# Decode attention and GLU on one core: whole-tile loads of K and V, an 80 KB K buffer with alternating places, and filler products on TensorE

## The chip, the cores and the metric

The kernel runs on one core of a Trainium2 chip. The metric is the device time of one execution in microseconds (us). The core has five engines that run their own instruction streams and wait for one another through semaphores: TensorE (PE in the profile; PEld is its weight load), VectorE (DVE), ScalarE (ACT), GpSimd (POOL) and SyncE (SP), which here issues nearly all of the transfers from HBM to SBUF. Sixteen DMA engines carry the transfers.

## The reference

One decode step of a transformer block, for one token with 640 features (bf16):

```python
h  = x + attention(layernorm(x)) @ wo       # 32 heads of 128, 4096 cached keys and values per head
h2 = h + (gelu(ln(h) @ w_gate) * (ln(h) @ w_up)) @ w_down      # hidden width 1728
```

`attention` computes q = layernorm(x) @ wq, the scores q.k / sqrt(128) against each head's 4096 cached keys, a softmax, and the weighted sum of the cached values. K and V are 32 x 4096 x 128 bf16 each, 33.6 MB, so that the two caches make up 67 of the 84 MB that the kernel reads. Each value is used once.

## The kernel before

**Tiles.** The 32 heads are worked on in four tiles (j = 0 to 3, `NG = 4`) of eight heads. In a tile every one of the 128 partitions holds 256 consecutive rows (keys) of one head, 64 KB; sixteen partitions make one head. A tile has two halves (s = 0, 1) of 128 rows, and each half two quarters (i = 0, 1) of 64 rows. `HALF` is the number of elements of a half in one partition.

**Buffers.** `k_all` holds one K tile: 64 KB in each partition. `v_all` holds one V tile. The weights share these two buffers: wq lies in `v_all` at the start; after the caches, `wo` lies at the start of `k_all` and w_down (`wd_sb`) behind it, w_gate and w_up in `v_all`.

**The order on SP.** Transfers are issued by SP in a list that is written out by hand, each behind its own wait: wq; K0 in two halves; V0 (when the q projection has read wq); then per tile the next K's first half (when `mults[j, 0, 1]`, the second multiplication of this tile, has read the first half), its second half (when `mults[j, 1, 1]` has), and the next V (when `pvs[j, 1]`, the last product with this V, is done). V3 is issued in two halves. Behind them come wo in two halves of 2.6 MB (when `mults[3, 1, 1]` is done), eight small loads into `wd_lo`, w_gate (when `pvs[3, 1]` is done), w_up, and w_down in four pieces.

**A tile on the engines.** q is broadcast to all partitions in `qb`. `mult(j, s, i)` multiplies a quarter of K with q on VectorE (L393, 64 x 128 products per partition, written to `prod[:, i]`). `fold(e, i)` lets TensorE add up groups of eight products by sixteen products with the identity `id_b` (L369 and, with the weights left loaded, the helper `held`, L167); i = 0 fills two PSUM banks, i = 1 two others. `total(j, s)` reduces the remaining sixteen on VectorE (L399) to the scores `sc`; ScalarE takes the exponential (L401) to `pt`; `block(j, s)` spreads it on VectorE to a block-diagonal weight `p_bd` (L406); `pv(e, s)` multiplies with V by 32 products (L381). Folds alternate between the two halves of `prod`, so the third multiplication waits for the first fold, and the third fold for the first reduction, which frees its PSUM banks.

VectorE's order in a tile is: mult, mult, mult, total, mult, block, total, block. TensorE's is a hardware loop over the tiles: `f00`, `f01`, `f10`, `f11`, `p0`, `p1`, `h`. Here `p0` waits for the first `p_bd` half and for V, `p1` for the second `p_bd` half and for `seen[j]`, a one-element memset on GpSimd (L437) that waits for V's second part; `h` sums over the partitions of a head (L387), after ScalarE's copy L443.

**The end.** After the last `h` the softmax sums are applied (L452 to L458), then the output projection with wo runs as two groups of 80 one-column products (L486), one for each half of wo; then the second layernorm, gate and up (L516, 75 one-column products each), the gelu chain on VectorE (L522 to L530), and the product with w_down (L539). At the start of TensorE's stream and near the end of VectorE's, `idle` puts NoOps (56 and 3).

The softmax here doesn't subtract the row's maximum and nothing guards it: scores larger than these inputs give would overflow.

## Time and profile before

| what | us |
|---|---|
| median of 3 runs (lowest, highest) | 202.18 (202.15, 202.31) |
| the profiled execution: its time | 202.28 |
| its span, first to last instruction | 200.9 |
| TensorE busy / VectorE busy / ScalarE busy | 115.3 / 103.6 / 9.4 |
| transfers: 84.23 MB, mean rate | 419 GB/s |
| mean granted TensorE clock | 0.795 |

A page's row gives a group of instructions: its line, engine, what it writes from what, how many there are and how long one takes, and how long the engine had been idle before them and what ended that. In a timeline a line has the start, the time from the first to the last of the merged instructions, the engine and the line, and in brackets the idle time before it. The chain of waits follows the work that ended last back to the start, and is printed in order of time.

### The profile page before, as it was taken

The numbers are of one execution on the slowest core, as the hardware profiler recorded it, in microseconds if no ns is written. First come the engines' busy times: TensorE is split into PE (matmuls) and PEld (weight loads), VectorE is DVE, ScalarE is ACT, GpSimd is POOL, SyncE is SP. The second block draws the span as 40 slices with busy tenths as digits, with TensorE's granted clock in tenths as the row PEclk, the third lists the DMA queues.
The fourth block names the chain that finished last, engine by engine and source line by source line (L and its number), as shares of the span: only waits on it lengthen the run. The fifth ranks groups of instructions, "written<-read, shape, count | busy, mean of one in ns | idle before, by whom it ended". The sixth has DMA issues, their size and how long they took to land.

```text
span 200.9 us, 2025 instructions
## 1 busy us (share of the span) xinstructions
PE 115.3 (57%) x982; PEld 30.4 (15%) x738; DVE 103.6 (52%) x56; ACT 9.4 (5%) x27; POOL 6.7 (3%) x36
## 2 busy tenths in 40 slices
PE   0108019667094296696605938566088496674675
PEld 0103000000032000001300000023000001474574
DVE  0200197994601969945149799420798965120320
ACT  2100000000001000000100000001000000100100
POOL 6500000000000000000000000000000000000000
PEclk9999856999858559579965899969669879955555
DMA  8999999999899999999999999899999999999992
GB/s 326 449 406 437 431 450 424 417 431 499 385 444 417 424 522 417 417 417 411 417 424 424 489 457 444 378 411 424 424 450 437 431 444 391 432 436 414 423 402 107
DMA packets 3275, 84.31 MB, mean 420 GB/s; under 512 B 387, under 2 KB 582, under 8 KB 966
## 3 DMA queue, kind: packets, MB, share of 16 engines
q1 hardware_dynamic: 3266, 84.23, 97.8%
q8 instruction: 4, 0.07, 0.1%
q14 instruction: 1, 0.01, 0.0%
q10 hardware_dynamic: 4, 0.00, 0.0%
HBM read 84.23 MB, written 0.00 MB: 419 GB/s over the span
## 4 chain that ended last, share of the span: by engine, by line
DMA 66%; DVE 22%; PE 11%; issue 0%; ACT 0%; SPq 0%; DVEq 0%
DMA k_all<-in_A_k_cache_dram 56%; DVE prod L393 18%; DMA v_all<-in_B_w_up_dram 10%; PE psum L167 7%; DVE sc L399 3%; PE psum L516 1%; PE psum L539 1%; PE psum L381 1%; DVE p_bd L406 1%; PE psum L369 1%; SPq L59 0%; ACT pt L401 0%; ACT out_row L555 0%; DVE hm L530 0%; DVEq L114 0%
## 5 line engine op out<-in xcount | busy, mean ns | idle before, releaser
L393 DVE TENSOR_TENSOR prod<-k_all,qb 128x8192 bf16<-128x8192 bf16 x16 | 70.4, 4421 | 38.0 <-DMA k_all<-in_A_k_cache_dram 33.1
L167 PE MATMUL psum<-prod,id_b 128*128 128x512 bf16 x240 | 66.0, 437 | 0.0
L369 PE MATMUL psum<-prod,id_b 128*128 128x512 bf16 x16 | 7.3, 454 | 45.3 <-DVE prod L393 31.5
L381 PE MATMUL psum<-v_all,p_bd 128*32 128x512 bf16 x256 | 19.4, 464 | 14.2 <-DMA v_all<-in_A_v_cache_dram 11.0
L399 DVE TENSOR_REDUCE sc<-psum 128x128 f32<-128x2048 f32 x8 | 18.3, 2288 | 13.3 <-PE psum L167 13.3
L369 PEld LDWEIGHTS psum<-prod,id_b 128*128 128x128 bf16 x16 | 1.6, 99 | 99.8 <-DVE prod L393 59.4
L381 PEld LDWEIGHTS psum<-v_all,p_bd 128*32 128x32 bf16 x256 | 7.5, 114 | 38.5 <-DMA v_all<-in_A_v_cache_dram 21.8
L406 DVE TENSOR_TENSOR p_bd<-pt,own 128x1024 bf16<-128x1024 bf16 x8 | 9.8, 1222 | 2.2 <-ACT pt L401 2.2
L401 ACT ACTIVATE pt<-sc,zero_t 128x128 bf16<-128x128 f32 x8 | 3.2, 402 | 135.9 <-DVE sc L399 135.9
L352 PE MATMUL psum<-v_all,xlnB 128*32 128x512 bf16 x40 | 4.5, 631 | 6.7 <-DMA v_all<-in_A_wq_dram 6.7
L486 PE MATMUL psum<-aP,k_all 128*128 128x1 bf16 x160 | 6.7, 178 | 2.7 <-DMA k_all<-in_A_wo_dram 2.7
L486 PEld LDWEIGHTS psum<-aP,k_all 128*128 128x128 bf16 x160 | 6.6, 131 | 2.8 <-DMA k_all<-in_A_wo_dram 2.8
L516 PE MATMUL psum<-hlnT,v_all 128*128 128x1 bf16 x150 | 5.5, 173 | 1.2 <-DMA v_all<-in_B_w_up_dram 1.2
L387 PE MATMUL psum<-hs,po_sb 128*128 128x8 f32 x32 | 4.2, 258 | 3.2 <-ACT po_sb L443 3.2
L437 POOL MEMSET spare<- 1x1 f32 x4 | 0.4, 88 | 162.8 <-DMA v_all<-in_A_v_cache_dram 162.8
L361 DVE CAST qb<-psum 128x512 bf16<-128x512 f32 x1 | 0.7, 692 | 9.7 <-PE psum L352 9.7
L516 PEld LDWEIGHTS psum<-hlnT,v_all 128*128 128x128 bf16 x150 | 5.3, 120 | 1.8 <-DMA v_all<-in_B_w_up_dram 1.3
L492 DVE COPY hT<-psum 128x5 f32<-128x5 f32 x1 | 0.2, 166 | 9.6 <-PE psum L486 9.6
L387 PEld LDWEIGHTS psum<-hs,po_sb 128*128 128x128 f32 x32 | 3.9, 191 | 5.1 <-issue 5.1
L323 PE MATMUL psum<-one_bf,x_row 1*128 1x1 bf16 x5 | 0.4, 177 | 7.1 <-DMA x_row<-in_A_x_dram 7.1
L326 DVE COPY xx<-psum 128x5 f32<-128x5 f32 x1 | 0.2, 165 | 7.5 <-PE psum L323 7.5
L443 ACT COPY po_sb<-psum 128x512 f32<-128x512 f32 x4 | 2.3, 585 | 22.3 <-PE psum L381 22.3
(71 smaller groups left out, 28.6 us busy)
## 6 DMA issues: line engine op xcount, KB each, us to landing
k_all<-in_A_k_cache_dram SPq DMA_DIRECT2D x8, 4096.0 KB, 29.1
v_all<-in_A_v_cache_dram SPq DMA_DIRECT2D x2, 4096.0 KB, 28.5
v_all<-in_A_wq_dram SPq DMA_DIRECT2D x1, 5120.0 KB, 15.2
k_all<-in_A_wo_dram SPq DMA_DIRECT2D x2, 2560.0 KB, 17.4
v_all<-in_B_w_gate_dram SPq DMA_DIRECT2D x1, 2160.0 KB, 15.0
v_all<-in_B_w_up_dram SPq DMA_DIRECT2D x1, 2160.0 KB, 19.8
k_all<-in_B_w_down_dram SPq DMA_DIRECT2D x1, 800.0 KB, 22.3
k_all<-in_B_w_down_dram SPq DMA_DIRECT2D x1, 640.0 KB, 20.9
```

Source lines behind the costliest of these rows:

```text
L167: built = e.matmul(out, lhsT, rhs, start=start, stop=stop)
L352: i = e.matmul(ps_q[32 * t:32 * t + 32, :], xlnB[:, c, 32 * a:32 * a + 32], wq_j[:, c, t, a, :, :], start=(c == 0 and a == 0), stop=(c == ...
L369: mm = held if n or not first else lambda e, *a, **k: e.matmul(*a, **k)
L381: i = e.matmul(ps_o[a:a + 32, :], p_bd[:, s, 4 * b:4 * b + 4, :].rearrange("p g j -> p (g j)"), vt[:, 4 * b:4 * b + 4, :], start=(s == 0 a ...
L387: i = e.matmul(ps_a[:, bass.ds(at, 8)], po_sb[:, 128 * r:128 * r + 128], hs[:, r, :], start=(r == 0), stop=(r == 3))
L393: mults[j, s, i] = VM(lambda e: e.tensor_tensor(out=prod[:, i, :, :], in0=kt[:, 64 * i:64 * i + 64, :], in1=qb[:, j, :].unsqueeze(1).to_br ...
L399: reds[j, s] = VR(lambda e: e.reduce_sum(sc[:, :], ps_f.rearrange("p (g d) -> p g d", d=16), axis=AX.X), folds[j, s, 1], exps.get((j, 0) i ...
L401: exps[j, s] = AS(lambda e: e.activation(pt[:, :], sc[:, :], ACTF.Exp, bias=zero_t[:, 0:1], scale=INV_SQRT_DH, accum_out=RS[:, 2 * j + s:2 ...
L406: blocks[j, s] = VB(lambda e: e.tensor_tensor(out=p_bd[:, s, :, :], in0=pt[:, :].unsqueeze(2).to_broadcast([128, 128, 8]), in1=own8[:, :]. ...
L443: evs[j] = AS(lambda e: e.copy(po_sb[:, :], ps_o), pvs[j, 1])
L486: r = e.matmul(ps_p[:, c:c + 1], wo_sb[:, i, c::5], aP[:, i:i + 1], start=False, stop=(i == 31), skip_group_check=True)
L516: i = e.matmul(ps[:, m:m + 1], ws, hlnT[:, c:c + 1], start=(c == 0 and m == 0), stop=(c == 4), skip_group_check=True)
```

## The change

- `k_all` becomes 80 KB in each partition. A K tile is loaded whole, in one transfer of 64 KB per partition: even tiles to rows 0 to 255 of the buffer, odd ones to rows 64 to 319. It is issued when the third multiplication of the tile before is done.
- Even tiles take their quarters in the order 2, 3, 1, 0, odd ones 0, 1, 2, 3, so that after three quarters all that the next tile overwrites has been read. In even tiles the second half's reduction is therefore two instructions of half the size.
- Every V tile is one transfer, the last one too, issued after the last V product of the tile before. The memsets `seen` go, and `p0` and `p1` run together after the second `p_bd`.
- `warm` adds products of a zero tile to a PSUM bank that is free: 8 when a K tile has landed, 12 between the second and the third fold, and 14 between the fourth fold and the products with V. They are 512 columns wide.
- wo is issued after the second multiplication of the last tile, instead of the last one.
- The NoOps on TensorE go from 56 to 22, those on VectorE go.

```diff
-    k_all = sb("k_all", [128, 2 * 128 * DH], BF16)
+    k_all = sb("k_all", [128, 320 * DH], BF16)
...
-    def load_k(j, s):
+    K_AT = [0, 64 * DH, 0, 64 * DH]
+
+    def load_k(j):
         src = A_k_cache[0, 8 * j:8 * j + 8, :, :].rearrange("h (p r) d -> (h p) (r d)", p=16)
-        landed["K", j, s] = P.dma("sync", k_all[:, HALF * s:HALF * s + HALF], src[:, HALF * s:HALF * s + HALF],
-                                  mults.get((j - 1, s, 1)))
+        landed["K", j] = P.dma("sync", k_all[:, K_AT[j]:K_AT[j] + 2 * HALF], src, mults.get((j - 1, 1, 0)), chan="K")
...
+    def load_v(j, *after):
+        landed["V", j] = P.dma("sync", v_all[:, 0:2 * HALF], src, *after, chan="V")
...
-    idle("tensor", 56)
+    idle("tensor", 22)
...
+    def warm(e, n, load=False):
+        for k in range(n):
+            mm = e.matmul if load and k == 0 else lambda *a, **kw: held(e, *a, **kw)
+            r = mm(ps_z, none_b[:, :], none_b[:, :].unsqueeze(1).to_broadcast([128, 4, 128]), start=True, stop=True)
         return r
...
     def mult(j, s, i):
-        kt = tile3(k_all[:, HALF * s:HALF * s + HALF])
+        c = (2 * s + i) if j % 2 else (2 + i, 1 - i)[s]
+        kt = tile3(k_all[:, K_AT[j]:K_AT[j] + 2 * HALF])
...
-            landed["K", j, s], qa, folds.get((j, 0, i) if s else (j - 1, 1, i)))
+            landed["K", j], qa, folds.get((j, 0, i) if s else (j - 1, 1, i)))
...
+        if s and j % 2 == 0:
+            V(lambda e: e.reduce_sum(sc[:, 64:128], g16(0, 1024), axis=AX.X), folds[j, s, 1], free)
+            reds[j, s] = VR(lambda e: e.reduce_sum(sc[:, 0:64], g16(1024, 2048), axis=AX.X))
+        else:
+            reds[j, s] = VR(lambda e: e.reduce_sum(sc[:, :], g16(0, 2048), axis=AX.X), folds[j, s, 1], free)
...
     lp = P.loop("tensor", range(NG), [
+        ("wa", lambda e, j: warm(e, 8, True), lambda j: [landed["K", j]], False),
         ("f00", lambda e, j: fold(e, 0), lambda j: [mults[j, 0, 0], reds[j - 1, 1] if j else qa], True),
         ("f01", lambda e, j: fold(e, 1), lambda j: [mults[j, 0, 1]], True),
+        ("wb", lambda e, j: warm(e, 12), lambda j: [], False),
         ("f10", lambda e, j: fold(e, 0), lambda j: [mults[j, 1, 0], reds[j, 0]], True),
         ("f11", lambda e, j: fold(e, 1), lambda j: [mults[j, 1, 1]], True),
-        ("p0", lambda e, j: pv(e, 0), lambda j: [blocks[j, 0], landed["V", j, 0]], True),
-        ("p1", lambda e, j: pv(e, 1), lambda j: [blocks[j, 1], seen[j]], True),
+        ("wc", lambda e, j: warm(e, 14), lambda j: [], False),
+        ("p0", lambda e, j: pv(e, 0), lambda j: [blocks[j, 1], landed["V", j]], True),
+        ("p1", lambda e, j: pv(e, 1), lambda j: [], True),
...
     for j in range(NG):
         mult(j, 0, 0)
         mult(j, 0, 1)
+        mult(j, 1, 0)
         if j < NG - 1:
-            load_k(j + 1, 0)
-        mult(j, 1, 0)
+            load_k(j + 1)
         total(j, 0)
         mult(j, 1, 1)
-        if j < NG - 1:
-            load_k(j + 1, 1)
         block(j, 0)
         total(j, 1)
         block(j, 1)
...
-        seen[j] = GS(lambda e: e.memset(spare[:, :], 0.0), landed["V", j, 1])
+        if j < NG - 1:
+            load_v(j + 1, pvs[j, 1])
...
-    d_wo = [... mults[NG - 1, 1, 1])
+    d_wo = [... mults[NG - 1, 0, 1])
             for i in (0, 16)]
...
-    idle("vector", 3)
```

## The prediction

> **What bounds the kernel now.** I read the page first (transfers, then the chain), then the timeline of the last tile, because the whole-span shares hide where a limit changes.

> The page's transfer rows and its queue table:

> ```profile
> DMA  8999999999899999999999999899999999999992
> q1 hardware_dynamic: 3266, 84.23, 97.8%
> ```

> The 16 engines are busy in every slice but the last; 84.23 MB are the whole input. The chain of waits says the same near its end (start, duration, what):

> ```profile
> 124.58 27.28 DMA k_all<-in_A_k_cache_dram
> ...
> 151.88 4.42 DVE prod L393
> 156.30 2.21 DVE sc L399
> ...
> 173.61 0.34 SPq L59
> ...
> 173.99 19.78 DMA v_all<-in_B_w_up_dram
> ```

> The last K half lands at 151.85; a compute path leads from there to the release of v_all (173.61), where the gate load is issued; then a transfer sets the pace again. Next the timeline, which shows how much room that compute path has:

> ```profile
> 142.17 8.76 DVE L393 TENSOR_TENSOR prod<-k_all,qb 128x8192 bf16<-128x8192 bf16 x2 [9.82 <-DMA k_all<-in_A_k_cache_dram]
> ...
> 151.88 4.42 DVE L393 TENSOR_TENSOR prod<-k_all,qb 128x8192 bf16<-128x8192 bf16 x1 [0.95 <-DMA k_all<-in_A_k_cache_dram]
> 156.22 2.29 DVE L399 TENSOR_REDUCE sc<-psum 128x128 f32<-128x2048 f32 x1
> 158.42 4.42 DVE L393 TENSOR_TENSOR prod<-k_all,qb 128x8192 bf16<-128x8192 bf16 x1
> ...
> 171.66 1.91 PE L381 MATMUL psum<-v_all,p_bd 128*32 128x512 bf16 x32 [2.42 <-DVE p_bd L406]
> 173.61 0.34 SPq L59 DMA_DIRECT2D v_all<-in_B_w_gate_dram  x1
> ...
> 177.53 3.33 PE L486 MATMUL psum<-aP,k_all 128*128 128x1 bf16 x80
> 183.53 3.36 PE L486 MATMUL psum<-aP,k_all 128*128 128x1 bf16 x80 [2.67 <-DMA k_all<-in_A_wo_dram]
> ...
> 193.82 2.75 PE L516 MATMUL psum<-hlnT,v_all 128*128 128x1 bf16 x75 [1.21 <-DMA v_all<-in_B_w_up_dram]
> ```

> The first two multiplications of tile 3 run at 142.17 on the first half of K, before the second half lands. After the last product with V (173.57) the rest waits only twice for a transfer: 2.67 us for the second half of wo and 1.21 us for up. So **the compute path at the end has 3.9 us of room**; without those waits it takes 27.3 (173.57 to the span's end, 200.9) - 3.9 = 23.4 us.

> [...] A full-clock fold of 16 products takes 3.62 us (0.216 each); at 0.5 ten take 4.00 us.

> **The change part by part**, for the last tile first. All bytes and their order in the queue stay, so the whole K3 lands when its second half did, at 151.85. What moves is tile 3's first two multiplications: they now wait for the whole tile, 9.71 us later. The new path, each duration from the rows above (two multiplications in 8.76, so 4.38 each in a row; a reduction 2.20 to the next start):

> - mult 1, 2, 3: 151.88 + 3 x 4.38 = 165.02. The third needs fold 1, which runs from 156.4 and at full clock ends at 160.0, before mult 2 does (160.64).
> - reduction 165.02 to 167.22, mult 4 to 171.64. Fold 3 (167.3 to 171.0) is hidden under it.
> - from a fourth mult's end to its p_bd, warm, tile 2 gives the time:

> ```profile
> 120.13 4.42 DVE L393 TENSOR_TENSOR prod<-k_all,qb 128x8192 bf16<-128x8192 bf16 x1
> ...
> 124.61 0.39 PE L369 MATMUL psum<-prod,id_b 128*128 128x512 bf16 x1 [0.64 <-DVE prod L393]
> 124.83 3.40 PE L167 MATMUL psum<-prod,id_b 128*128 128x512 bf16 x15
> 128.27 2.29 DVE L399 TENSOR_REDUCE sc<-psum 128x128 f32<-128x2048 f32 x1 [2.59 <-PE psum L167]
> ...
> 131.12 1.22 DVE L406 TENSOR_TENSOR p_bd<-pt,own 128x1024 bf16<-128x1024 bf16 x1 [0.56 <-ACT pt L401]
> ```

>  124.55 to 132.34 is 7.8 us: p_bd is done at 179.4.
> - Both V halves now follow it: 0.14 + 2 x 1.91 = 4.0 us, end 183.4. Before, p0 ran ahead of the last reduction; 1.9 of the delay is this.

> So v_all is free at 183.4 instead of 173.57: **9.8 us later**, against 3.9 us of room. Then 23.4 us: span 206.8 for 200.9, **+5.9 us**.

> Transfers at the end: the gate load, and everything queued behind it on SP (up, four w_down loads), is issued at 183.45. The second wo half lands about then (183.5), so the engines, which ran on, now pause. The output's own small DMA takes 1.0 us from issue to landing; with the completion of wo as much again, I estimate a pause of 1.5 to 3 us. Gate, up and w_down follow their old spacing (188.6, 193.8, 198.9), 2 us later: 190.6, 195.8, 200.9. Compute wants them at 197, 199.9 and 203.5. **The pause is hidden**; up to 2.6 us more would be too.

> Middle tiles, if the queue is never empty there: K(j+1) is issued 13.2 us after K(j) lands (three multiplications), V(j) lands 19.4 us after it. V(j+1) is issued 31.6 us after K(j), K(j+1) lands after 39. Room of 6 and 7 us; a cold first fold takes 2. So I cost them at nothing; the cover is the transfer already queued.

> Fills: no row shows products with the zero tile; price per piece 0.216 (full) to 0.43 (half), by the folds. Fill a (8) takes 3.4 us cold, under mult 1 (4.4). Fill b (12) 2.6 us, from 164.3 to 166.9, just before fold 3 at 167.3. Fill c (14) 3.0 us, 175.2 to 178.2, before p0 at 179.5. Warm, they delay nothing. Their worth is the clock: at best, every fold as above. At worst they do not raise it: fold 1 up to 2.1 later, fold 3 past mult 4 by 1.2, fill c 1.7 over, V products 6.5 (as at 54.92) instead of 3.9, +7.6 together. I take the full clock, and 0.3 for a late rise in fold 1.

> At nothing: two reductions for one in even tiles (about 0.1 us more, under the room above); 34 fewer NoOps on TensorE (the projection waits for wq until 15.27, xlnB is done at 10.1); the three NoOps on VectorE (its copy waited 2.42 anyway); the POOL memsets and five SP issues that go (no engine's bound); wo's earlier release (V3 is still ahead in the queue until 171.3); V3 in one piece (needed at 179.5).

> **Sum.** Span 200.9 + 5.9 + 0.3 = 207.1. The profiled execution took 202.28 with its span of 200.9, so 208.5; it stood 0.1 above the median of 202.18: **208.4**.

> **The rivals.**
> - *Fills do not hold the clock* (0.12). For: their operand is zero, and no row shows what counts as busy. Against: the gaps that they fill are where it fell. +2 to +7.6 on the sum: 210 to 216, middle 212.
> - *The clock stays up in the tail* (0.08). Output projection, GLU and down products (6.7, 5.5, 2.3 us) ran at 0.5; the projection now runs as one 6.7 us burst. All at double speed saves 7.2 us, but then w_down's landing at 200.9 sets the end, plus 2.0 us as before: 204.3. Against: 75 one-column products in a row left the clock at 0.5.
> - *A transfer gap in the middle* (0.05): a cold tile eats the 6 us room and K or V is issued late; +1 to +3, 209.5 to 211.5.
> - *Faster transfers, so not slower* (0.05). Whole-tile loads move faster and K3 lands earlier. It decides from 6 us, a landing at 145.9: 63.96 MB at 440 GB/s instead of 422, giving 202 or a little less. [...]
> - The forecast (0.70): 207.3 to 209.6.

> **How the numbers follow.** The likeliest case gives 208.4. The range runs from 206.5 (part of the tail fast) to 211.5 (middle gaps, fills half effective), leaving out the worst of the fills and the two low ends. A measurement here tells apart about 0.2%, 0.4 us; the only case near or below that is the fourth: faster 0.03, same 0.02, slower 0.95.

> **What would show it.** In the new profile: tile 3's first multiplication at 151.9 and none before; four of them with one reduction between; the last V product near 183.4; no transfer wait before the output projection; DMA below 9 tenths near 183 to 186; gate and up landed before their products. Wrong if K3 lands elsewhere than 151 to 153, if folds of the last tile take over 4.5 us (clock), if the one-column products take under 35 ns each, or if an engine waits for K for over 40 us between tiles.

## The result, and the profile after

The changed kernel takes **208.83 us** (median of 6 runs, 207.41 to 209.44) against 202.22 us before (6 runs, 202.15 to 202.31): 1.032 times as long, 95% interval 1.028 to 1.035. It is slower by 6.6 us. The profiled execution took 208.79 us with a span of 207.5.

The page of the changed kernel, its transfer rows and the queue:

```profile
DMA  9999999999999999999999999999999999839980
q1 hardware_dynamic: 2546, 84.23, 94.8%
```

The same 84.23 MB; the slices are full up to the 34th, then there is a hole in the next two, and the last slice carries next to nothing. The transfers no longer run to the end. The chain of waits of the changed kernel, its last part (start, duration, what):

```profile
125.98 25.55 DMA k_all<-in_A_k_cache_dram
...
151.56 4.44 DVE prod L400
...
156.65 4.97 PE psum L167 x15
...
161.64 4.43 DVE prod L400
...
180.45 3.67 PE psum L384 x64
...
188.02 6.46 PE psum L496 x160
...
197.49 5.28 PE psum L526 x150
...
202.81 0.46 issue
203.27 0.18 DVE hm L540
```

From the landing of K3 to the end there is no transfer in it any more. Before, a transfer of 19.8 us, up behind gate, stood in the chain shortly before the end; now the output projection (L496) runs its 160 products in one piece, gate and up (L526) their 150. The timeline of tile 3 shows where the time went:

```profile
151.56 8.76 DVE L400 TENSOR_TENSOR prod<-k_all,qb 128x8192 bf16<-128x8192 bf16 x2 [11.21 <-DMA k_all<-in_A_k_cache_dram]
...
156.44 5.16 PE L167 MATMUL psum<-prod,id_b 128*128 128x512 bf16 x15
...
161.64 4.43 DVE L400 TENSOR_TENSOR prod<-k_all,qb 128x8192 bf16<-128x8192 bf16 x1 [1.32 <-PE psum L167]
...
168.18 4.42 DVE L400 TENSOR_TENSOR prod<-k_all,qb 128x8192 bf16<-128x8192 bf16 x1
...
180.45 3.64 PE L384 MATMUL psum<-v_all,p_bd 128*32 128x512 bf16 x64 [1.15 <-DVE p_bd L419]
184.13 0.34 SPq L59 DMA_DIRECT2D v_all<-in_B_w_gate_dram  x1
```

All four multiplications stand behind K3's landing, where before two had been done by then. The third waited 1.32 us for the first fold, which ran mostly at half clock (granted clock 0.50 in the window from 156 to 160; 16 products in 5.6 us instead of 3.6). The gate load is issued at 184.13 instead of 173.61: 10.5 us later.

### The profile page after: what moved, and what is told of

It is laid out like the page before. It is cut to its first block, busy times and chain, and to the rows that moved or that the text cites. A ratio compares the mean times of both kernels' runs of the same rounds, so it can differ in the third digit from the quotient of the medians.

```text
span 207.5 us, 2113 instructions
## 1 busy us (share of the span) xinstructions
PE 139.0 (67%) x1118; PEld 29.7 (14%) x742; DVE 103.6 (50%) x58; ACT 9.4 (5%) x27; POOL 7.4 (4%) x32
## 3 DMA queue, kind: packets, MB, share of 16 engines
q1 hardware_dynamic: 2546, 84.23, 94.8%
HBM read 84.23 MB, written 0.00 MB: 406 GB/s over the span
## 4 chain that ended last, share of the span: by engine, by line
DMA 53%; DVE 27%; PE 18%; issue 1%; ACT 1%; SPq 0%; DVEq 0%
DMA k_all<-in_A_k_cache_dram 53%; DVE prod L400 23%; PE psum L167 7%; PE psum L496 3%; PE psum L526 3%; DVE sc L412 2%; PE psum L384 2%; PE psum L547 1%; PE psum L366 1%; DVE p_bd L419 1%; PE psum L390 1%; DVE hX L510 0%; PE psum L506 0%; PE psum L327 0%; ACT po_sb L453 0%
## 5 line engine op out<-in xcount | busy, mean ns | idle before, releaser
L167 PE MATMUL psum<-prod,id_b 128*128 128x512 bf16 x240 | 58.4, 399 | 0.0
L167 PE MATMUL psum<-none_b 128*128 128x512 bf16 x132 | 36.2, 430 | 0.0
L373 PE MATMUL psum<-none_b 128*128 128x512 bf16 x4 | 2.4, 608 | 30.9 <-DMA k_all<-in_A_k_cache_dram 30.9
L384 PE MATMUL psum<-v_all,p_bd 128*32 128x512 bf16 x256 | 14.5, 380 | 4.7 <-DVE p_bd L419 4.7
L412 DVE TENSOR_REDUCE sc<-psum 128x128 f32<-128x2048 f32 x6 | 13.7, 2286 | 5.2 <-PE psum L167 5.2
L366 PE MATMUL psum<-prod,id_b 128*128 128x512 bf16 x16 | 6.6, 415 | 10.1 <-DVE prod L400 7.8
L384 PEld LDWEIGHTS psum<-v_all,p_bd 128*32 128x32 bf16 x256 | 6.5, 97 | 37.1 <-DVE p_bd L419 30.9
L455 POOL TENSOR_TENSOR RT<-RS,own 128x64 f32<-128x64 f32 x1 | 1.3, 1325 | 170.9 <-ACT pt L413 170.9
L496 PE MATMUL psum<-aP,k_all 128*128 128x1 bf16 x160 | 6.6, 178 | 0.0
L496 PEld LDWEIGHTS psum<-aP,k_all 128*128 128x128 bf16 x160 | 6.5, 131 | 0.0
L526 PE MATMUL psum<-hlnT,v_all 128*128 128x1 bf16 x150 | 5.3, 173 | 0.0
L526 PEld LDWEIGHTS psum<-hlnT,v_all 128*128 128x128 bf16 x150 | 5.2, 120 | 0.5 <-DVE hlnT L513 0.5
L409 DVE TENSOR_REDUCE sc<-psum 128x64 f32<-128x1024 f32 x2 | 2.4, 1224 | 5.2 <-PE psum L167 5.2
## 6 DMA issues: line engine op xcount, KB each, us to landing
v_all<-in_B_w_up_dram SPq DMA_DIRECT2D x1, 2160.0 KB, 13.8
```

Source lines behind the costliest of these rows:

```text
L167: built = e.matmul(out, lhsT, rhs, start=start, stop=stop)
L366: mm = held if n or not first else lambda e, *a, **k: e.matmul(*a, **k)
L373: r = mm(ps_z, none_b[:, :], none_b[:, :].unsqueeze(1).to_broadcast([128, 4, 128]), start=True, stop=True)
L384: i = e.matmul(ps_o[a:a + 32, :], p_bd[:, s, 4 * b:4 * b + 4, :].rearrange("p g j -> p (g j)"), vt[:, 4 * b:4 * b + 4, :], start=(s == 0 a ...
L412: reds[j, s] = VR(lambda e: e.reduce_sum(sc[:, :], g16(0, 2048), axis=AX.X), folds[j, s, 1], free)
L496: r = e.matmul(ps_p[:, c:c + 1], wo_sb[:, i, c::5], aP[:, i:i + 1], start=False, stop=(i == 31), skip_group_check=True)
```

## The experiments

All times are medians beside runs of the kernel before on the same chip (202.17 to 202.25 us in each group).

**K3 in two halves again, all else as changed.** It separates the last tile from the rest of the change.

```diff
-landed["K", j] = dma(K tile j, whole)
+landed["K", j], landed["K2", j] = K tile j whole for j < 3; K3 as two loads of HALF
-    mult(j, s, i): waits landed["K", j]
+    mult(j, s, i): waits landed["K2" if s else "K", j]
```

> The changed kernel with one part undone: K3 alone is again loaded in two halves, so that the first two multiplications of tile 3 need only the first half. Tiles 0 to 2, the fills and the joined V products stay as changed. Theory (the loss is the 9.7 us by which the first two multiplications of the LAST tile start later, less the room at the end): first half at 141.9, third multiplication at 151.6, then 4.4 + 2.2 + 4.4 + 7.8 + 3.7 us, last V product done near 174.1, inside the room; transfers set the end again: 202.2, from 201.8 to 202.6, against 208.8. Rival (the loss sits in the whole-tile loads of all tiles, or in the fills, or in the joined V products): it stays at 206 or more.

Measured: 202.06 us (20 runs, 201.88 to 204.31; 17 of them under 202.6), ratio to before 1.000 (0.999 to 1.002). The timeline of this kernel:

```profile
142.02 8.76 DVE L406 TENSOR_TENSOR prod<-k_all,qb 128x8192 bf16<-128x8192 bf16 x2 [0.26 <-DMA k_all<-in_A_k_cache_dram]
...
175.09 0.34 SPq L59 DMA_DIRECT2D v_all<-in_B_w_gate_dram  x1
...
183.31 3.36 PE L502 MATMUL psum<-aP,k_all 128*128 128x1 bf16 x80 [1.11 <-DMA k_all<-in_A_wo_dram]
...
193.65 2.77 PE L532 MATMUL psum<-hlnT,v_all 128*128 128x1 bf16 x75 [1.29 <-DMA v_all<-in_B_w_up_dram]
```

Two multiplications start at 142.0 again, and the two transfer waits of the end are back. The last V product ends 1.5 us later than before, inside the room; that is 1.0 us later than expected, because VectorE waited 1.8 us for the first fold, which stood on TensorE behind tile 2's products with V and the fillers. The 0.26 in the first line says how close this is: whole-tile loads make tile 2's own work end later, 0.26 us before the first half of K3 lands. So the loss goes when K3 alone comes in halves; whole-tile loads in tiles 0 to 2, the 80 KB buffer, the fillers and the joined V products then cost nothing together, since they fit into the room. Nor do they gain: transfers set the end, as before.

**The kernel before, with only K3 loaded whole.**

```diff
+if j == NG - 1: landed["K", j, 0] = landed["K", j, 1] = dma(K tile j, whole), issued after mults[j - 1, 1, 1]
```

> The kernel before with K3 alone loaded whole, in one transfer, when tile 2's fourth multiplication is done; nothing else of the change. Theory: tile 3's four multiplications start at 151.9, its first fold is cold (5 to 6 us) and holds up the third one by 1.3 to 2 us; the V products still run in two pieces, which saves 1.9 us against the changed kernel; last V product near 183 to 184 instead of 173.6, less 3.9 us of room: 207 to 209. Rival (a whole K3 alone is absorbed, the loss needs the other parts too): under 205.

Measured: 208.80 us (4 runs, 208.60 to 210.13), ratio 1.035 (1.031 to 1.038). Its timeline:

```profile
151.74 8.76 DVE L397 TENSOR_TENSOR prod<-k_all,qb 128x8192 bf16<-128x8192 bf16 x2 [16.99 <-DMA k_all<-in_A_k_cache_dram]
...
162.03 4.43 DVE L397 TENSOR_TENSOR prod<-k_all,qb 128x8192 bf16<-128x8192 bf16 x1 [1.53 <-PE psum L167]
...
180.93 3.51 PE L385 MATMUL psum<-v_all,p_bd 128*32 128x512 bf16 x32 [2.42 <-DVE p_bd L410]
184.47 0.34 SPq L59 DMA_DIRECT2D v_all<-in_B_w_gate_dram  x1
```

So loading K3 whole is enough for the loss, and undoing it is enough to end it. That the two times are nearly equal is in part chance, since the paths differ: this kernel gains what the split V products give (32 instead of 64 behind the last p_bd), and loses it again, because without fillers those 32 ran mostly at half clock (0.50 from 182 to 184) and took 3.51 us, against 1.91 before.

**The kernel before, with the V products joined.**

```diff
-("p0", lambda e, j: pv(e, 0), lambda j: [blocks[j, 0], landed["V", j, 0]], True),
+("p0", lambda e, j: pv(e, 0), lambda j: [blocks[j, 1], landed["V", j, 0]], True),
```

> The kernel before, with the first 32 V products of every tile held back until the second p_bd is done, as the changed kernel does; K loads as before, no fills. Theory of the room: the last V product ends 1.9 us later, 175.5, which is less than the 3.9 us of transfer waits behind it: same time, 202.0 to 202.5. The waits for wo and up shrink by about 1.9 us in all. Rival (every delay of the last V product is a delay of the end, since the gate load is released by it): 204.

Measured: 202.28 us (12 runs): eight of them lie from 202.08 to 202.31, four from 204.21 to 204.74; ratio of all 1.004 (1.001 to 1.007). In the profiled run (202.11) the gate load was issued at 176.29, 2.7 us later than before (the V products ran partly at half clock: the page's slice from 170.8 to 175.8 has 6 tenths, and 64 took 5.2 us), the wait for wo was gone, and the up products still waited 1.19 us for their load. So in eight of the twelve runs a delay of this kind cost nothing: the room is real, and 1.2 us of it were left. What carried four runs past it was not seen in a profile.

**The gate load earlier, into the free part of the K buffer.**

```diff
-wg_sb = v_all[:, 0:5 * DF]            d_wg waits pvs[NG - 1, 1]
+wg_sb = k_all[:, 226 * DH:226 * DH + 5 * DF]    d_wg waits mults[NG - 1, 1, 1]; d_wu waits pvs[NG - 1, 1]
```

> The changed kernel with w_gate loaded into the part of the 80 KB K buffer that w_down leaves free, when tile 3's fourth multiplication is done (172.6) instead of the last V product (184.1); up still waits for the V buffer. Theory (compute sets the end, the transfer pause at 180 to 186 is hidden): the pause shrinks to under 1 us, gate and up land 2 us earlier or more, and the time stays that of the changed kernel, 207.4 to 209.4. Rival (the pause is a part of the loss): 2 us or more less, 206.8 or below.

Measured: 208.60 us (4 runs, 207.04 to 209.15), ratio 1.030 (1.025 to 1.035), the time of the changed kernel. The windows, first of the changed kernel, then of this one (last three columns: clock, DMA share, GB/s):

```profile
180.00:182.00 2.00, 1.55 (x32) 0.78 (x36) 0.40 (x1) 0.00 (x0) 0.55 (x1) 1.00 0.46 184
182.00:184.00 2.00, 2.00 (x40) 0.82 (x32) 0.00 (x0) 0.00 (x0) 0.00 (x0) 1.00 0.00 0
184.00:186.00 2.00, 1.21 (x14) 1.13 (x11) 0.00 (x0) 0.59 (x1) 0.00 (x0) 1.00 0.62 130
```

```profile
180.00:182.00 2.00, 1.93 (x36) 1.00 (x40) 0.01 (x1) 0.00 (x0) 0.16 (x1) 1.00 1.02 428
182.00:184.00 2.00, 1.71 (x32) 0.66 (x24) 0.00 (x0) 0.24 (x1) 0.00 (x0) 1.00 0.99 424
184.00:186.00 2.00, 1.51 (x12) 1.41 (x12) 0.00 (x0) 0.34 (x1) 0.00 (x0) 1.00 1.01 432
```

In the changed kernel the engines lie idle for 1.1 + 2.0 + 0.8 = 3.8 us; here not at all. The time doesn't move beyond its spread: the pause is hidden.

**Without the fillers.**

```diff
-("wa", ... warm(e, 8, True) ...), ("wb", ... warm(e, 12) ...), ("wc", ... warm(e, 14) ...)
```

> The changed kernel without the filler products (8, 12 and 14 per tile); all else as changed. Theory: the first fold of a tile is no colder than it mostly is with them (5 to 6 us), fold 3 stays fast, but the 64 V products start at half clock after 4 us of idling and take 5 us or more instead of 3.6: 1.5 us later, 210, from 209 to 211.5. Rival (fills with a zero operand do not move the clock): unchanged, 208.8, with the same durations of folds and V products. Second rival (fills are in the way of the real products): under 208.

Measured: 212.64 us (4 runs, 212.15 to 212.87), ratio 1.052 (1.050 to 1.054), so without the fillers the changed kernel is 3.8 us slower; I had expected about 1, and at most 211.5. All V products ran partly at half clock (granted clock 0.59 and 0.56 in the two windows from 180 to 184, against 1.00 in the changed kernel), as the timeline of this kernel shows:

```profile
66.05 6.13 PE L384 MATMUL psum<-v_all,p_bd 128*32 128x512 bf16 x64 [4.31 <-DVE p_bd L419]
...
103.32 6.26 PE L384 MATMUL psum<-v_all,p_bd 128*32 128x512 bf16 x64 [4.25 <-DVE p_bd L419]
...
142.78 5.32 PE L384 MATMUL psum<-v_all,p_bd 128*32 128x512 bf16 x64 [4.31 <-DVE p_bd L419]
...
180.87 5.05 PE L384 MATMUL psum<-v_all,p_bd 128*32 128x512 bf16 x64 [4.25 <-DVE p_bd L419]
...
205.22 0.84 PE L523 MATMUL psum<-hlnT,v_all 128*128 128x1 bf16 x20 [1.33 <-issue]
```

The profiled run is 3.4 us longer than that of the changed kernel. 1.4 us is the slower products of tile 3. 0.8 is K3 landing later (first multiplication at 152.34, not 151.56): V1 was issued at 72.22, only 1.8 us ahead of K1's landing, instead of 6.4, and by K2 the transfers were 0.75 us behind (113.61 for 112.86). 0.4 comes off, because the third multiplication waited 0.88 us for the first fold, not 1.32. 1.33 is a stall of TensorE amid the up products, with nothing to wait for. So 1.8 of the 3.4 us follow from the clock; whether the stall has to do with the fillers is not shown.

**24 more fillers ahead of every K.**

```diff
+("w0", lambda e, j: warm(e, 24, True), lambda j: [], False),
 ("wa", lambda e, j: warm(e, 8, True), lambda j: [landed["K", j]], False),
```

> The changed kernel with 24 more filler products at the start of every tile, ahead of the wait for K, so that TensorE does not idle between the last V product of one tile and the next K. Theory (the 0.7 us by which the change is slower than my sum, and its spread from 207.4 to 209.4, are the first fold of tile 3 at half clock, which held up the third multiplication by 1.3 us): first fold 3.6 us, no wait of VectorE for TensorE there, 207.3, all runs within 0.6 us. Rival (the spread comes from elsewhere): it stays at 207.4 to 209.4 with the same spread.

Measured: 208.36 us (4 runs: 207.56, 207.77, 208.94, 209.04), ratio 1.031 (1.027 to 1.035). In the profile (207.77) the clock was 1.00 in every window from 144 to 184, the first fold of tile 3 took 3.6 us and the third multiplication did not wait. The spread stayed, which speaks against the cold fold as its cause. It doesn't rule it out, since no run near 209 was profiled; the mean granted clock of those two, 0.909 and 0.919, was no lower than the 0.908 and 0.915 of the two faster ones.

**The last tile's V products split again.**

```diff
-lp = P.loop("tensor", range(NG), [...])
+lp = P.loop("tensor", range(NG - 1), [...])     # tile 3 written out: ..., f11, p0 after blocks[3, 0], p1 after blocks[3, 1]
```

> The changed kernel with tile 3 written out behind a loop of three tiles, so that there the first 32 V products run when the first p_bd is done, under the last reduction, in place of the 14 fillers; all else as changed. Theory (joining the V products put half of them, 1.8 us, on the path): last V product near 182.2 instead of 184.1, 206.9, with the same spread of 1 us to both sides. Rival (the V products run cold when the 14 fillers are gone, and give it back): 208 to 209.

Measured: 208.12 us (5 runs, 206.46 to 208.44), ratio 1.029 (1.027 to 1.031). In the profiled run, the fastest, the gate load was issued at 180.78, 29.44 us after the first multiplication of tile 3, against 31.2 in another profile of the changed kernel whose fold was warm too (below): 1.7 us less, as argued. TensorE stalled for 1.0 us in the up products here:

```profile
178.83 1.91 PE L384 MATMUL psum<-v_all,p_bd 128*32 128x512 bf16 x32 [2.33 <-DVE p_bd L419]
180.78 0.34 SPq L59 DMA_DIRECT2D v_all<-in_B_w_gate_dram  x1
...
199.31 1.14 PE L543 MATMUL psum<-hlnT,v_all 128*128 128x1 bf16 x28 [1.00 <-issue]
```

Most of the gain did not reach the median. The other four runs had a mean granted clock of 0.82 to 0.83, against 0.88 in the profiled one, so the clock may have taken it; no profile of them shows where.

**Fillers in the tail.**

```diff
+("wd", lambda e, j: warm(e, 3, True), lambda j: [], False),     # ahead of "h"
+T(lambda e: warm(e, 4, True, ps_s))                             # after z_sum
```

> The changed kernel with filler products in TensorE's short waits between the last V product and the output projection too (3 before the head sum of every tile, 4 after the softmax sums), so that the clock is still full when the projection's 160 one-column products start at about 188. It tells whether the clock staying up in the tail could give the loss back. Forecast: the clock falls within 5 us of the last filler, since one-column products do not hold it; while it is up they run no faster than 30 ns each, instead of 41: 0.5 to 1.5 us less, 207.3 to 208.3. Rival (the clock rival of the prediction): the projection keeps the clock up, projection, GLU and down products run at double speed, 204.5. Second rival: one-column products do not depend on the clock, 208.8.

Measured: 207.38 us (4 runs, 207.26 to 207.58), ratio 1.025 (1.024 to 1.027). The windows of the output projection's products alone (busy and number on PE and PEld, then clock, DMA share, GB/s):

```profile
186.50:188.50 2.00, 2.00 (x50) 2.00 (x51) 1.00 1.01 432
...
190.00:192.00 2.00, 2.00 (x55) 2.00 (x53) 0.50 1.03 432
```

The count of a window takes in the products that are under way at its start, four or five of them, since one takes 178 ns here and about 41 ns pass from one to the next; at 186.5 there were none yet. So 50 at full clock and 55 at half clock mean about the same rate. The timelines say it more exactly, the changed kernel first, whose projection ran at half clock (0.50 in the windows from 188 to 196):

```profile
187.90 6.57 PE L496 MATMUL psum<-aP,k_all 128*128 128x1 bf16 x160
```

```profile
186.49 6.80 PE L498 MATMUL psum<-aP,k_all 128*128 128x1 bf16 x160
```

With the first half of the products at full clock they took 42.5 ns each on average, with none of them 41.1. So no run shows the 30 ns that the forecast had for a product at full clock. The one-column products of the projection gained nothing from the clock, and 160 of them did not hold it: it was 1.00 from 188 to 189.5 and 0.50 from 190, so it fell some 3 us after the first. That the median is lower by 1.4 us can't be put down to a faster projection; in this profile the first fold simply did not wait.

**The three NoOps of VectorE put back, on top of the tail fillers.**

```diff
+idle("vector", 3)
 def down(ms, qs=range(4)):
```

> The changed kernel with the tail fillers (whose runs lay close together, 207.26 to 207.58), and with the three NoOps of the kernel before put back on VectorE behind the step that writes hm. In the kernels without them hm started 0.5 us after the last up product where compute sets the end, in the kernels that keep them 0.1 us. Theory (the NoOps shift where in its instruction stream VectorE stalls; my prediction costed them at nothing and was 0.4 us off there): hm 0.1 us after the last up product, 207.0, from 206.8 to 207.2. Rival (the 0.4 us come from elsewhere, the NoOps are worth nothing): 207.4, hm still 0.5 us after.

Measured: 208.35 us (4 runs, 207.55 to 209.32), ratio 1.032 (1.027 to 1.036), and hm started 0.53 us after the last up product, as without them. The theory falls: the NoOps are worth nothing here. The narrow spread of the kernel with tail fillers did not come back, and with four runs of each it may have been chance.

**The changed kernel and the 24 fillers once more, one profile each.**

> The changed kernel once more, for one profile beside its time: what differs between its executions of 207.4 and of 209.4. Theory: the wait of VectorE for the first fold of tile 3 (1.3 us in the profile shown) goes from 0 to some 2 us, and the time minus that wait is 207.4 in every profile. Rival: the wait is the same and something else has moved (the landing of K3, or stalls in the tail).

> The same once more, a third profile of the changed kernel: time minus the wait of VectorE for the first fold of tile 3 is 207.4 again, if that wait makes the spread; not so, if something else does.

> The kernel with 24 fillers ahead of every K once more, for a second profile: its runs spread from 207.6 to 209.0 although no first fold waited in its first profile (207.77). Theory: some executions still start the tile cold, and then the fillers themselves run at half clock (10 us for 24 instead of 5) and push the first fold back: a time near 209 goes with a wait of VectorE for the first fold, a time near 207.6 with none. Rival: near 209 without such a wait.

Measured: 207.97 and 207.86 us for the changed kernel, 207.65 for the other. The timelines of the first of these and of the third:

```profile
151.86 13.10 DVE L400 TENSOR_TENSOR prod<-k_all,qb 128x8192 bf16<-128x8192 bf16 x3 [9.72 <-DMA k_all<-in_A_k_cache_dram]
```

```profile
151.35 13.10 DVE L400 TENSOR_TENSOR prod<-k_all,qb 128x8192 bf16<-128x8192 bf16 x3 [10.06 <-DMA k_all<-in_A_k_cache_dram]
```

Three multiplications in a row, no wait for a fold. Without the wait 207.9, with 1.32 us of it 208.8: the wait accounts for the difference of the profiled runs, less 0.3 because K3 landed later and 0.2 in the tail. So "207.4 in every profile" was off by 0.5. No execution near 209.4 was caught in a profile; what makes those stays open. A cold fold is not an obvious answer, since the run of 209.44 had the highest mean granted clock of the six, 0.870. The runs of 208.9 and 209.0 with 24 fillers may well be the same.

## Why the prediction was right

The forecast was 208.4, from 206.5 to 211.5; measured 208.83. The mechanism held. That the number is within 0.4 us is partly luck: the runs spread over 2 us, and the errors of the terms nearly cancel. By its own steps, in the profiled execution:

- **The place and the path: right.** That the whole K3 lands where its second half did was my estimate, from the unchanged bytes and order of issue; it landed at 151.56 (151.88 forecast), and all four multiplications stood behind it. Undoing that one load gives the time of before back; doing that one alone gives the time of after, by a somewhat different path.
- **The path's length: right.** From the start of the third multiplication to the last p_bd 18.75 us, forecast 18.76, with each duration taken from a row of before. The V products took 3.7 instead of 4.0: both halves run in one piece.
- **The allowance for a cold first fold: too small in this execution.** Forecast 0.3 (up to 2.1); measured 1.32 in the profile shown and 0 in two others. No run shows the 0.3, which was my estimate; before, the first folds of the four tiles took 5.6, 6.2, 5.6 and 5.0 us, 1.4 to 2.6 above the 3.6 at full clock. Fill a runs under the first multiplication, but it started at half clock itself and didn't raise it in time here (0.50 in the windows from 148 to 160). A fold of the last tile over 4.5 us was on the prediction's own list of signs of being wrong, and this one took 5.6; the sum had the full clock for it, and the 0.3.
- **The room of 3.9 us and the tail of 23.4: right.** From the last V product to the end 23.4 us. Delays of 1.5 and 2.7 us were absorbed in two experiments, with one run of twenty and four of twelve some 2 us longer.
- **The pause of the transfers: hidden, as said, but mis-sized.** Forecast 1.5 to 3 us, measured 3.8. The second half of wo landed at 183.1 (183.5 forecast), but the share of busy transfer engines fell from about 180.5 on and was nothing from 182, so a pause counted from the landing comes out too short. (The profile with 24 more fillers, its gate load issued at 182.61, has 2.2 in the three windows from 180 to 186.) Gate landed at 192.7 and up at 198.3 (issue plus 8.6 and 13.8), 2 us or more later than I had them. Up was needed near 200.1, so 1.8 us of cover were left, not 4.
- **The middle tiles: nothing, as costed**, with the fillers there: V1 was issued 6.4 us ahead of K1's landing. Without them 1.8 us were left and 0.75 us lost, as the rival of a gap in the middle had it.
- **The rivals.** Before, the clock was at 0.52 and 0.50 in the two windows from 64 to 72 and at 0.50 from 104 to 108 and from 144 to 148, each time after a tile's last V product. Fillers with a zero operand did raise it: the mean granted clock was 0.774 to 0.833 in the runs without them, 0.835 to 0.870 in those of the changed kernel, 0.908 to 0.919 with 24 more. The clock in the tail was no lever for the projection: pricing a full clock at half of the products' time was wrong for its 6.7 us, since they ran no faster there (42.5 ns each for 41.1). Gate, up and down ran at half clock before, in the changed kernel and in every experiment down to the tail fillers, so their part of the 7.2 us is not tested. Larger loads landed hardly earlier: K3's first multiplication came at most 0.5 us sooner in any profile (151.34 for 151.88).

The sum's errors, -0.3 for the landing, +1.0 for the fold, -0.3 for the V products, make the 0.4 between 207.1 and 207.5.

No version beats the kernel before: with K3 in halves the rest of the change is at its time, since the same 84.23 MB of transfers set the end in both, at a mean of 419 and 420 GB/s.

## What to carry to other kernels

Where transfers set the time, as here, a larger load was free only as long as the work behind its landing fitted into the room at the end: with K3 in halves the last V product ended 1.5 us later, inside 3.9 us of room, and the time stayed (202.06 us); with K3 whole it ended 10.5 us later, and the time rose to 208.83. So cost the last tile separately, from its landing to the last instruction, with the transfer waits counted as room. Load the last tile in pieces even where whole tiles are right for all others. A stop of the transfers that showed in a row of the page was no loss here, since nothing waited for what came late: the kernel with the early gate load closed the 3.8 us of it and took 208.60 us for 208.83.
